# Zeros on GpSimd, later loads, and alternating products of r in an attention and expert kernel

## Chip, cores and metric

The kernel runs on one core of a Trainium2 chip. The metric is the time of one execution on the device in microseconds (us), as the median of several runs.

## The reference

First a recurrence over 768 steps for 4 x 8 heads of width 40, then an elementwise product of two projections with a third projection behind it:

```python
for t in range(S):
    y[:, :, t] = np.einsum('bhd,bhde->bhe', rt, state)
    Sa = np.einsum('bhde,bhe->bhd', state, at)
    state_decay = state * wt[:, :, None, :] - np.einsum('bhd,bhe->bhde', Sa, bt)
    state = state_decay + np.einsum('bhd,bhe->bhde', vt, kt)
...
a = x @ w_a        # 3072 x 320 by 320 x 1536
b = x @ w_b
return (a * b @ w_out).astype(np.float32)
```

The weights of the second part come as 64-bit floats, so the kernel decodes their words into a high and a low 32-bit part.

## The kernel before

The 768 steps are cut into 12 chunks n of 64 steps; each chunk has two halves c of the heads, numbered q = 2n + c. The stages of attention are:

- **Preparation** (`prep`, L512) of one q: loads of W, BK and A; two scans on VectorE (DVE), Q and pe, with a reciprocal between them; BK and A are multiplied by them; `scores` on TensorE (PE, L564), whose results go to AB (copied by ScalarE, ACT) and through a mask to TK (DVE); transposes of BK (`nat`, L599); and stores of A, pe, TK and bkn to a scratch tensor un_d in DRAM.
- **Lanes** (`lanes`, L611) for a pair of chunks, six times: a DVE transpose of AB into N, 31 dependent pairs of DVE instructions on Y that invert 32 x 32 triangles, and two transposes out, TC and T3.
- **Merge** (`merge`, L643) of one chunk: two rounds of 32 x 32 products (l2a, l2b) that complete the inverse T.
- **Main** (`main`, L696) of one q: loads of un (from un_d), SV and rv; the products r (`r_`, L721), u, s, g and y in a chain through ACT and DVE. The state ST runs from s of one chunk to r of the next, so this chain is serial over the chunks. r has 16 products: 128 rows deep, 64 stationary columns, 40 moving ones, written to one of two halves of the output's partitions (`half(j)`). s (`s_`, L757) has 16 of the same depth and moving width, with 40 stationary columns, and changes the half with each product.

The second part is cut into 12 slices of the 1536 inner columns. A **unit** (L416) is one slice times one chunk's 256 tokens: sixteen products into ab, a copy by ACT to asb, a product g by DVE, the split of g into gh (ACT) and gl (GpSimd, POOL), and six products into po. Four slices (F1) are worked while attention runs, eight after it. Each slice needs three weight pieces; a piece is loaded to one of two buffers wraw, decoded by six DVE, two ACT and two POOL instructions (L333), and written to a slot.

All instructions of this part are first recorded by a planner (`Plan`, L77) as operations with an engine, a cost, the keys that they read and write, and a due time v. `Plan.run` (L118) then walks through time and, on the engine that can start earliest, takes the ready operation that is due first. What it emits is kept in that order on each engine's queue: the keys set the order, while real waits come from the data. All DMAs are issued by SP, one queue in program order, with eight outstanding at most. Before the change the weights' loads read no key and the loads of SV and rv in `main` neither, so they are ready at time 0.

Ahead of the plan, L497 and L498 set zeros on DVE in AB, the two T, the two ST, the two RH and D1. tmp (L491) takes the sum of s and the old state before the decay is multiplied into ST.

Of the kernel before, what the change touches and what calls it, by code (L numbers as in the profile page):

```python
# [32 lines left out]
CW = M * CP  # L33
F1 = 4
# [31 lines left out]
class Op:  # L66
    __slots__ = ("eng", "dur", "fn", "deps", "users", "v", "lat", "need", "free", "mode", "end", "left", "ready", "seq", "moved")


class Banks:  # L70


    def __init__(self, n):
        self.n, self.ids = n, None


class Plan:  # L77
# [8 lines left out]
    def op(self, eng, dur, fn, r=(), w=(), v=None, lat=0.07, need=None, free=(), mode=None, moved=0.0):  # L86
        o = Op()
        o.moved = moved
# [29 lines left out]
    def run(self, slack=0.05, switch=0.13):  # L118
# [3 lines left out]
        last_mode = None  # L122
        ready = {e: [] for e in engines}
# [8 lines left out]
        while todo:  # L132
# [29 lines left out]
            if o.eng == "PE":  # L162
                if o.mode != last_mode:
                    d += switch
                last_mode = o.mode
            engines[o.eng] = s + d
# [94 lines left out]
def wkv_moe(ctx, tc, wd, ai, bk, rvf, vn, pin, rv, wa, wb, wo, out):  # L261
# [23 lines left out]

    def transp(ps, x):
        nc.tensor.matmul(ps, lhsT=x, rhs=ident, start=True, stop=True, is_transpose=True)
# [29 lines left out]
    pl = Plan(4)  # L317

    def us(n, fixed=0.16, each=0.00106):
        return fixed + each * n  # L320

# [9 lines left out]
    temps = [[stage.tile([P, NG * P], I32, name=f"w_{x}{i}") for x in ("ex", "mt", "rs")] for i in range(2)]  # L331

    def decode(i, src, rows, ncol, dst_hi, dst_lo, split):  # L333
# [3 lines left out]
        ex, mt, rs = (x[:rows, 0:ncol] for x in temps[i % 2])  # L337
# [4 lines left out]
        K, kr = [("w", i % 2, x) for x in ("ex", "mt", "rs")], ("raw", i % NR)  # L342
# [56 lines left out]
    def plan_tile(f, w, slot, v):  # L399
        for i, j, (eng, dur, fn, r, wr, lat) in tile_steps(f, w):  # L400
# [5 lines left out]
            pl.op(eng, dur, fn, r, wr, v=v, **kw)  # L406
# [6 lines left out]
          for x in ("asb", "g", "gh", "gl")}  # L413
    nunit = 0

    def unit(xk, kx, w, slot, first, last, done, v):  # L416
# [4 lines left out]
        ab, (asb, g, gh, gl) = AB2[i], (mo[x][i] for x in ("asb", "g", "gh", "gl"))  # L421
# [8 lines left out]
        for j in range(2):  # L430
            pl.op("PE", 0.95, lambda j=j: half(j), [kx] + wk, [("ab", i)], v=v, mode="r", lat=0.1)
# [7 lines left out]
        def second():  # L439
            for hf in range(2):  # L440
# [7 lines left out]
              v=v - 0.2, mode="r", lat=0.1)  # L448
# [18 lines left out]
    TK_ = ring(pp, 1, [P, 2, 4, C], "TK")  # L467
    PE_ = ring(pp, 2, [P, M, CP], "pe")
    BN_ = ring(pp, 1, [P, M, 2, D], "bkn")
# [21 lines left out]
    tmp = a1.tile([P, 4, 2, D], F32, name="tmp")  # L491
# [5 lines left out]
    for t in (AB, *T_, *ST_, *RH_, D1):  # L497
        nc0.vector.memset(t, 0.0)  # L498
# [13 lines left out]
    def prep(n, c, v):  # L512
        q = n * NP + c
        s2, x = q % 2, place[n]
        W, Q, BK, A, TK, PEt, BN = W_[s2], Q_[s2], BK_[s2], A_[s2], TK_[0], PE_[s2], BN_[0]
        kW, kQ, kBK, kA, kTK, kPE, kBN = ("W", s2), ("Q", s2), ("BK", s2), ("A", s2), ("tk", 0), ("pe", s2), ("bn", 0)
# [16 lines left out]
        pl.op("DVE", us(2 * M * C), lambda: nc.vector.tensor_mul(  # L533
# [7 lines left out]
        pl.op("DVE", us(M * C), lambda: nc.vector.tensor_mul(out=A, in0=A, in1=PEt[:, :, 0:C]), [kPE], [kA])  # L541
# [31 lines left out]
        pl.op("PE", 1.15, scores, [kBK, kA], need=ps, mode="q", lat=0.1, w=[("sc", q), kAB, kTK])  # L573
# [22 lines left out]
        for k in range(2):  # L596
# [8 lines left out]
            pl.op("PE", 0.5, nat, [kBK], need=ps, mode="t", lat=0.1, w=[("nt", q, k), (*kBN, k)])  # L605
# [37 lines left out]
    def merge(n, x, v):  # L643
# [25 lines left out]
        pl.op("PE", 1.15, l2a, kab + [("T3", x)], [("l3", n), "W4"], need=ps, mode="h", lat=0.1)  # L669
# [13 lines left out]
        pl.op("PE", 1.15, l2b, ["W4", ("TC", x)], [("l4", n), kT[2]], need=ps, mode="h", lat=0.1)  # L683
# [6 lines left out]

    def load_v(n, c, v):

        pl.dma(lambda: nc.sync.dma_start(out=SV_[c].rearrange("p g j i d -> p (g j i d)"), in_=vn[n, c]),
               [], [("svv", c), ("svs", c)], 1.1, v=v)
# [530 lines left out]
```

## Time and profile before

| | |
|---|---|
| three timed runs | 881.32, 872.25, 878.12 us; median 878.12 |
| the profiled execution | 881.76 us; span 879.8 us; mean granted TensorE clock 0.911 |
| busy share of the span | PE 83%, PE's weight loads 78%, DVE 68%, ACT 43%, POOL 26% |
| first transpose into N; last G of attention | 63.84 us; about 573 us |
| DMA | 156.58 MB, mean 178 GB/s |

In the page's slices each digit is the busy share of a fortieth of the span (22 us) in tenths. The chain of waits goes back from the last instruction to what released it, so its shares tell which engine the time was spent on when everything else waited. A window row sums busy time within a stretch. Nearly all instructions carry the line of one helper, L60, so groups are told apart by tile: "at<-SV,un 128*64 128x40" is the product r (128 rows, 64 stationary columns, 40 moving), "128*40" is s, "at<-A,BK" are the scores, "ab<-xk,wt" and "po<-wo" the unit's products, and w_ex, w_mt and w_rs the decode. PE shows two instructions for each fp32 product, so r has 32.

### The profile page before, as it was taken

Reading aid. Unit: us, or ns where it says so; the run is one execution under the profiler, and the core shown is the slowest. Engines: PE = TensorE matmul, PEld = TensorE weight load, DVE = VectorE, ACT = ScalarE, POOL = GpSimd, SP = SyncE. Lnnn points to the kernel's source line nnn. Section 1 sums busy time; section 2 is a strip of 40 time slices with the busy share of each in tenths; the row PEclk is TensorE's granted clock in tenths of the full one; section 3 lists DMA queues with packets and bytes.
Section 4 is the critical chain, followed back from the end, with each engine's and each line's share of the span. In section 5 each row is a group of like instructions: output and inputs, shape, how many; then the busy total and the mean of one; then the engine's idle time right before and its main releaser. Section 6 shows DMA issues by size and latency. Waiting matters only on the chain.

```text
span 879.8 us, 29127 instructions
## 1 busy us (share of the span) xinstructions
PE 728.7 (83%) x12538; PEld 684.8 (78%) x12538; DVE 594.3 (68%) x1162; ACT 379.8 (43%) x991; POOL 232.2 (26%) x265
## 2 busy tenths in 40 slices
PE   2453577788897898897989997799699999999996
PEld 2342466788787787787869886699699999999996
DVE  8979878969798798978658534874499822222222
ACT  3452473466535564644644453443244422222221
POOL 1310000244312011211112122455266622222222
PEclk9997588859996899989988999799899999999999
DMA  7897389768977878987775769579522100000111
GB/s 262 291 298 236 90 251 366 208 187 276 285 231 180 262 242 283 262 272 248 213 234 161 231 200 254 154 206 222 131 81 71 40 1 2 1 1 2 60 60 64
DMA packets 102018, 156.58 MB, mean 178 GB/s; under 512 B 30250, under 2 KB 70250, under 8 KB 98810
## 3 DMA queue, kind: packets, MB, share of 16 engines
q1 hardware_dynamic: 101882, 154.64, 58.3%
q8 instruction: 100, 1.64, 0.8%
q14 instruction: 36, 0.29, 0.1%
HBM read 101.97 MB, written 48.78 MB: 171 GB/s over the span
## 4 chain that ended last, share of the span: by engine, by line
PE 49%; DVE 26%; DMA 11%; issue 9%; ACT 3%; POOL 1%; SPq 0%; DVEq 0%; ACTq 0%; POOLq 0%
PE ab L60 20%; PE at L60 19%; PE po L60 9%; DVE Yt L60 5%; DVE Y L60 4%; DMA wraw<-in_wb_dram 3%; DVE w_ex L60 2%; DMA xk<-xk_d 2%; DVE w_mt L60 2%; DVE g L60 2%; DVE pe L60 1%; DVE w_rs L60 1%; DVE Q L60 1%; DMA wraw<-in_wa_dram 1%; DVE G L60 1%
## 5 line engine op out<-in xcount | busy, mean ns | idle before, releaser
L60 PE MATMUL ab<-xk,wt 120*128 120x256 f32 x2304 | 314.8, 290 | 15.1 <-issue 7.8
L60 PEld LDWEIGHTS ab<-xk,wt 120*128 120x128 f32 x2304 | 297.2, 196 | 18.1 <-issue 8.3
L60 POOL TENSOR_TENSOR gl<-g,gh 128x256 fp32r<-128x256 f32 x144 | 115.9, 805 | 403.8 <-ACT gh L60 399.5
L60 DVE TENSOR_TENSOR g<-ab,asb 128x256 f32<-128x256 f32 x144 | 60.5, 421 | 181.5 <-ACT asb L60 181.3
L60 PE MATMUL po<-wo,gh 128*128 128x320 f32 x576 | 156.8, 322 | 8.1 <-ACT gh L60 7.4
L60 ACT COPY asb<-ab 128x256 f32<-128x256 f32 x144 | 53.5, 372 | 155.5 <-PE ab L60 155.2
L60 PEld LDWEIGHTS po<-wo,gh 128*128 128x128 f32 x576 | 105.5, 194 | 11.0 <-ACT gh L60 8.4
L60 PE MATMUL po<-wo,gl 128*128 128x320 f32 x288 | 92.6, 322 | 3.2 <-POOL gl L60 3.2
L60 ACT CAST gh<-g 128x256 fp32r<-128x256 f32 x144 | 58.4, 406 | 78.4 <-DVE g L60 77.3
L60 PE MATMUL at<-SV,un 128*64 128x40 f32 (+1 forms) x1472 | 70.2, 232 | 15.8 <-ACT w_ex L60 4.6
L60 PEld LDWEIGHTS at<-SV,un 128*64 128x64 f32 (+1 forms) x1472 | 64.2, 142 | 23.1 <-ACT w_ex L60 5.0
L60 DVE TENSOR_TENSOR Y<-Y,Yt 128x31 f32<-128x31 f32 (+15 forms) x186 | 68.4, 368 | 6.4
L60 DVE TENSOR_TENSOR Yt<-Y,N 128x31 f32<-128x31 f32 (+15 forms) x186 | 67.7, 364 | 4.9
L60 PE MATMUL at<-ident,BK 128*128 128x128 f32 x192 | 36.0, 338 | 34.7 <-DMA rv<-in_rvf_dram 14.1
L60 PEld LDWEIGHTS po<-wo,gl 128*128 128x128 f32 x288 | 56.2, 195 | 6.2 <-POOL gl L60 5.8
L60 PEld LDWEIGHTS at<-ident,BK 128*128 128x128 f32 x192 | 27.2, 173 | 37.7 <-issue 19.6
L60 POOL TENSOR_TENSOR xk<-XF,xk 120x512 fp32r<-120x512 f32 (+1 forms) x24 | 34.1, 1443 | 65.0 <-ACT xk L60 64.6
L60 POOL TENSOR_TENSOR w_mt<-w_mt,wt 120x384 f32<-120x384 f32 x24 | 26.3, 1095 | 79.8 <-ACT wt L60 79.7
L60 PE MATMUL at<-A,BK 64*64 64x64 f32 x1536 | 38.2, 270 | 9.2 <-ACT bkn L60 6.8
L60 PEld LDWEIGHTS at<-A,BK 64*64 64x64 f32 x1536 | 34.5, 180 | 14.0 <-ACT bkn L60 8.4
L60 PE MATMUL at<-T,AB 32*32 32x32 f32 x768 | 18.6, 210 | 31.4 <-DVE T L60 26.1
L60 DVE TENSOR_TENSOR acc<-po,acc 128x320 f32<-128x320 f32 x96 | 42.3, 481 | 2.7 <-PE po L60 2.7
(84 smaller groups left out, 1131.1 us busy)
## 6 DMA issues: line engine op xcount, KB each, us to landing
un<-un_d SPq DMA_DIRECT2D x24, 1092.0 KB
BK<-in_bk_dram SPq DMA_DIRECT2D x24, 512.0 KB
rv<-in_rvf_dram SPq DMA_DIRECT2D x24, 512.0 KB
xk_d<-xk SPq DMA_DIRECT2D x11, 720.0 KB
xk<-xk_d SPq DMA_DIRECT2D x11, 720.0 KB
SV<-in_vn_dram SPq DMA_DIRECT2D x24, 320.0 KB
un_d<-bkn SPq DMA_DIRECT2D x24, 320.0 KB
W<-in_wd_dram SPq DMA_DIRECT2D x24, 260.5 KB
```

The source lines that it names most:

```text
L60: r = fn(*args, **kwargs)
```

## The change

- AB is not set to zero any more. The zeros of T, ST and RH are set by POOL, those of D1 stay on DVE.
- The weights' loads read a planner key that the second q's scores write (`WG`), and the first four slices are recorded behind the preparation and the lanes of the first pair. The loads of un, SV and rv for chunk 0 read the key N (`begun`), so they come behind the first transpose into N in the planner's time.
- r loops over i and gq outside and j inside, so that its products alternate between the two halves of the output.
- The planner gets a model of PE's clock: a 3.413 us window with less than 5100 columns of work makes the next one 1.85 times as long (`Clock`), and each PE operation gets its `work`. It moves instructions, and does nothing on the chip by itself.
- g takes the place of asb, and ST that of tmp.
- Of new settings NTK, NBN, NTMP, FILLERS and ON_POOL keep what was there before (one TK, one bkn, two sets of decode temporaries, no filler products, nothing of the preparation on POOL). One product with zeros into unused columns of PO, with its cast and its zeros on DVE, is new at the start.

```diff
+CLK, FILL, FILLC = 1, 0.6, 0.9
+WG = [("sc", 1)]
...
+class Clock:
+    WINDOW, ENOUGH, SLOW = 3.413, 5100, 1.85
...
+    def full(self, t):
+        return self.work.get(int(t / self.WINDOW) - 1, 0.0) >= self.ENOUGH
...
+                    d = clock.run(s, d, o.work) - s
...
+    fl = const.tile([P, P], F32R, name="fl")
+    nc0.vector.tensor_copy(out=fl, in_=ident)
+    fr = const.tile([P, 192], F32R, name="fr")
+    nc0.vector.memset(fr.bitcast(F32), 0.0)
...
+    mul(PO[0][:, 320:512], fl, fr)
...
-            pl.op(eng, dur, fn, r, wr, v=v, **kw)
+            pl.op(eng, dur, fn, list(r) + (WG if eng == "SP" else []), wr, v=v, **kw)
...
-        pl.op("ACT", 0.37, lambda: nc.scalar.copy(out=asb, in_=ab[:, 0, :]), [("ab", i)], [("asb", i)], v=v - 0.4)
-        pl.op("DVE", 0.42, lambda: nc.vector.tensor_mul(out=g, in0=ab[:, 1, :], in1=asb),
-              [("ab", i), ("asb", i)], [("g", i)], v=v - 0.4)
+        pl.op("ACT", 0.37, lambda: nc.scalar.copy(out=g, in_=ab[:, 0, :]), [("ab", i)], [("g", i)], v=v - 0.4)
+        pl.op("DVE", 0.42, lambda: nc.vector.tensor_mul(out=g, in0=ab[:, 1, :], in1=g),
+              [("ab", i)], [("g", i)], v=v - 0.4)
...
-    for t in (AB, *T_, *ST_, *RH_, D1):
-        nc0.vector.memset(t, 0.0)
+    nc0.vector.memset(D1, 0.0)
+    for t in (*T_, *ST_, *RH_):
+        nc0.gpsimd.memset(t, 0.0)
...
+    def begun(n):
+        return ["N"] if n == 0 else []
...
-        pl.dma(lambda: nc.sync.dma_start(out=UN, in_=un_d[q]), [("un", q, i) for i in range(5)], [kU], 3.7, v=v - 0.3)
+        pl.dma(lambda: nc.sync.dma_start(out=UN, in_=un_d[q]), [("un", q, i) for i in range(5)] + begun(n), [kU], 3.7, v=v - 0.3)
...
-            out=RV.rearrange("p x m t -> p (x m t)"), in_=rvf[n, c]), [], [kRV], 1.7, v=v - 0.2)
+            out=RV.rearrange("p x m t -> p (x m t)"), in_=rvf[n, c]), begun(n), [kRV], 1.7, v=v - 0.2)
...
-            for j in range(2):
-                for i in range(4):
-                    for gq in range(2):
+            for i in range(4):
+                for gq in range(2):
+                    for j in range(2):
                         k = mi(gq, i) * D
                         mul(bank(ps)[half(j), k:k + D], AK[:, gq, j, i], SV[:, gq, j, i])
...
-    for f in range(F1):
-        plan_tile(f, slots[f], f, wv[f])
...
+        if g[0] == 0:
+            for f in range(F1):
+                plan_tile(f, slots[f], f, wv[f])
```

The order on the engines moves with this. SP's queue behind the loads of the first two q, before the change (the digit behind a tile's name is its buffer, the last number only a running one):

```order
L60 DMA SV0_206<-in_vn_dram 128x640
L60 DMA rv0_208<-in_rvf_dram 128x1024
L60 DMA SV1_207<-in_vn_dram 128x640
L60 DMA rv1_209<-in_rvf_dram 128x1024
L60 DMA wraw0_159<-in_wa_dram 120x768
L60 DMA wraw1_160<-in_wb_dram 120x768
L60 DMA un_d0_126<-pe0_192 128x520
L60 DMA W0_181<-in_wd_dram 128x521
L60 DMA un_d0_126<-A0_189 64x2x256 x2
L60 DMA un_d0_126<-bkn0_194 128x640
L60 DMA BK0_187<-in_bk_dram 128x1024
L60 DMA un_d0_126<-TK0_191 64x2x256 x2
```

and with the change:

```order
L66 DMA un_d0_131<-pe0_195 128x520
L66 DMA W0_184<-in_wd_dram 128x521
L66 DMA un_d0_131<-A0_192 64x2x256 x2
L66 DMA A0_192<-in_ai_dram 128x512
L66 DMA un_d1_132<-pe1_196 128x520
L66 DMA BK0_190<-in_bk_dram 128x1024
L66 DMA un_d0_131<-TK0_194 64x2x256 x2
L66 DMA un_d0_131<-bkn0_197 128x640
L66 DMA un_d1_132<-A1_193 64x2x256 x2
L66 DMA W1_185<-in_wd_dram 128x521
L66 DMA un_d2_133<-pe0_195 128x520
L66 DMA un_d2_133<-A0_192 64x2x256 x2
```

The loads of chunk 0's SV and rv and the first two weight pieces have left the place behind the first six loads; the preparation's own stores and loads have moved up to it.

PE's queue around the first r, which before stood between the second and the third scores:

```order
L60 MATMUL at3_66<-ident_71,BK0_187 128x128 x4
L60 MATMUL at2_65<-ident_71,BK0_187 128x128 x4
L60 MATMUL at2_65<-SV0_206,un0_202 64x40 x16
L60 MATMUL at2_65<-A0_189,BK0_187 64x64 x2
L60 MATMUL at3_66<-A0_189,BK0_187 64x64 x2
L60 MATMUL at2_65<-A0_189,BK0_187 64x64 x2
```

With the change both r of chunk 0 stand behind the transposes that follow the fifth scores:

```order
L66 MATMUL at0_63<-ident_71,BK0_190 128x128 x4
L66 MATMUL at1_64<-ident_71,BK0_190 128x128 x4
L66 MATMUL at1_64<-SV0_209,un0_205 64x40 x16
L66 MATMUL at1_64<-SV1_210,un1_206 64x40 x16
L66 MATMUL at1_64<-A1_193,BK1_191 64x64 x2
L66 MATMUL at0_63<-A1_193,BK1_191 64x64 x2
```

The two r now follow each other and stand ahead of the sixth scores instead of ahead of the third and the fourth.

DVE's queue from the end of the first round of lanes, before:

```order
L60 STREAM_TRANSPOSE TC_199<-Y_197 128x32x32
L60 STREAM_TRANSPOSE T3_200<-Y_197 128x32x32
L60 SCALAR_TENSOR_TENSOR Q1_184<-W1_182,one_76 128x521
L60 TENSOR_TENSOR BK1_188<-BK1_188,Q1_184 128x1024
L60 TENSOR_SCALAR rp_186<-Q1_184 128x8
L60 RECIPROCAL d1_185<-rp_186 128x8
L60 SCALAR_TENSOR_TENSOR pe1_193<-W1_182,d1_185 128x520
L60 TENSOR_TENSOR A1_190<-A1_190,pe1_193 128x512
L60 TENSOR_SCALAR w_ex1_164<-wraw1_160 128x320
L60 TENSOR_SCALAR w_mt1_165<-wraw1_160 128x320
L60 TENSOR_SCALAR w_rs1_166<-wraw1_160 128x320
L60 SCALAR_TENSOR_TENSOR Q0_183<-W0_181,one_76 128x521
```

and with the change:

```order
L66 STREAM_TRANSPOSE TC_202<-Y_200 128x32x32
L66 STREAM_TRANSPOSE T3_203<-Y_200 128x32x32
L66 SCALAR_TENSOR_TENSOR Q1_187<-W1_185,one_81 128x521
L66 TENSOR_TENSOR BK1_191<-BK1_191,Q1_187 128x1024
L66 TENSOR_TENSOR TK0_194<-at2_65,tri_84 128x512
L66 TENSOR_SCALAR rp_189<-Q1_187 128x8
L66 RECIPROCAL d1_188<-rp_189 128x8
L66 SCALAR_TENSOR_TENSOR pe1_196<-W1_185,d1_188 128x520
L66 TENSOR_TENSOR A1_193<-A1_193,pe1_196 128x512
L66 SCALAR_TENSOR_TENSOR w_rs1_171<-w_rs1_171,w_ex1_169 120x384
L66 TENSOR_SCALAR w_ex0_166<-wraw0_164 128x320
L66 TENSOR_SCALAR w_mt0_167<-wraw0_164 128x320
```

Ahead of the first transpose into N stand 30 decode instructions before the change and 11 with it; behind the first round, up to the second transpose into N, four pieces and the end of another stand where there was one.

More of the change, by code (lines that the diff above doesn't have):

```diff
@@ L66 @@
 class Op:
-    __slots__ = ("eng", "dur", "fn", "deps", "users", "v", "lat", "need", "free", "mode", "end", "left", "ready", "seq", "moved")
+    __slots__ = ("eng", "dur", "fn", "deps", "users", "v", "lat", "need", "free", "mode", "end", "left", "ready", "seq", "moved", "work")
 class Banks:
@@ L74, in __init__, with run @@
         self.n, self.ids = n, None
+class Clock:
+    WINDOW, ENOUGH, SLOW = 3.413, 5100, 1.85
+    def __init__(self):
+        self.work = {}
+    def full(self, t):
+        return self.work.get(int(t / self.WINDOW) - 1, 0.0) >= self.ENOUGH
+    def run(self, t, d, work):
+        left = 1.0
+        while left > 1e-9:
+            k = int(t / self.WINDOW)
+            d1 = d if self.full(t) else d * self.SLOW
+            part = min(left, ((k + 1) * self.WINDOW - t + 1e-9) / d1)
+            self.work[k] = self.work.get(k, 0.0) + part * work
+            t += part * d1
+            left -= part
+        return t
 class Plan:
@@ L122, in run @@
         last_mode = None
+        clock = Clock()
         ready = {e: [] for e in engines}
@@ L165, in run @@
                 last_mode = o.mode
+                if CLK:
+                    t = engines["PE"]
+                    if self.filler and s - t > 0.4:
+                        share = FILL if clock.full(t) else FILLC
+                        nf = int(share * (s - t) / (0.09 if clock.full(t) else 0.17))
+                        for _ in range(nf):
+                            self.filler()
+                            t = clock.run(t, 0.09, 384)
+                        self.nfill = getattr(self, "nfill", 0) + nf
+                        s = max(s, t)
+                    d = clock.run(s, d, o.work) - s
             engines[o.eng] = s + d
@@ L412, in wkv_moe @@
     mo = {x: [mp.tile([P, 256], F32R if x in ("gh", "gl") else F32, name=f"{x}{i}") for i in range(2)]
-          for x in ("asb", "g", "gh", "gl")}
+          for x in ("g", "gh", "gl")}
     nunit = 0
@@ L420, in unit @@
         nunit += 1
-        ab, (asb, g, gh, gl) = AB2[i], (mo[x][i] for x in ("asb", "g", "gh", "gl"))
+        ab, (g, gh, gl) = AB2[i], (mo[x][i] for x in ("g", "gh", "gl"))
         wt, wot = w
@@ L762, in s_ @@
                             mul(bank(ps)[hd(j), c0:c0 + D], BN[:, mi(gq, i), j], SV[:, gq, j, i])
-            pl.op("PE", 0.75, s_, [kU, kS, kV], [("s", q), kST, "tmp"], need=ps, mode="c", lat=0.1)
+            pl.op("PE", 0.75, s_, [kU, kS, kV], [("s", q), kST], need=ps, work=2560, mode="c", lat=0.1)
             sv = ST[:, :, :, 0:D]
@@ L945, in wkv_moe @@
               + [(k, c) for k in ("svs", "svv", "rv", "rh", "st", "sd") for c in range(NP)]
-              + [("ut", 0), ("ut", 1), ("gm", 0), ("gm", 1), "tmp", ("x", 0)] + [("xf", 0, i) for i in range(3)])
+              + [("ut", 0), ("ut", 1), ("gm", 0), ("gm", 1), ("x", 0)] + [("xf", 0, i) for i in range(3)])
     def late():
@@ L1108, in all_tiles @@
             w = weight_tiles(p, "s")
[L1109 removed]
+            g, gh, gl = (mo[x][0] for x in ("g", "gh", "gl"))
             for f in range(NF):
@@ L1116, in all_tiles @@
                         mul(AB2[0][:, j, :], w[0][:, j, kw, :], xk[:, kxi, :], k == 0, k == 7)
-                nc.scalar.copy(out=asb, in_=AB2[0][:, 0, :])
-                nc.vector.tensor_mul(out=g, in0=AB2[0][:, 1, :], in1=asb)
+                nc.scalar.copy(out=g, in_=AB2[0][:, 0, :])
+                nc.vector.tensor_mul(out=g, in0=AB2[0][:, 1, :], in1=g)
                 nc.scalar.copy(out=gh, in_=g)
```

71 lines of the change are left out of this document (41 added, 30 removed).

## Prediction

> **What bounds the kernel now.** I read the page's slices first, then its chain of waits, then busy time by stage. The stage edges are events on VectorE (DVE): start of the first transpose into N, which opens the first round of lanes; end of the last transpose that closes it; the second transpose into N; the end of its round; the third transpose into N; the end of attention.
>
> ```profile
> PE   2453577788897898897989997799699999999996
> DVE  8979878969798798978658534874499822222222
> PE 49%; DVE 26%; DMA 11%; issue 9%; ACT 3%; POOL 1%; SPq 0%; DVEq 0%; ACTq 0%; POOLq 0%
> 0.00:63.80 63.80, 24.71 (x384) 21.82 (x388) 53.78 (x81) 26.04 (x66) 14.54 (x25) 1.00 0.86 282
> 63.80:98.00 34.20, 8.65 (x196) 7.16 (x189) 32.14 (x74) 8.74 (x20) 0.00 (x0) 0.70 0.56 178
> 98.00:128.10 30.10, 25.91 (x764) 23.34 (x764) 23.81 (x38) 21.44 (x59) 2.84 (x4) 0.67 0.69 196
> 128.10:165.20 37.10, 27.90 (x735) 24.54 (x734) 32.24 (x83) 16.24 (x45) 2.54 (x2) 0.90 0.91 316
> 165.20:228.10 62.90, 51.56 (x1196) 47.50 (x1194) 49.59 (x80) 33.46 (x88) 21.94 (x21) 0.76 0.79 234
> 228.10:573.00 344.90, 299.83 (x6983) 273.87 (x6981) 253.65 (x501) 174.50 (x468) 71.23 (x71) 0.90 0.77 231
> 573.00:879.80 306.80, 290.18 (x2300) 286.55 (x2300) 149.07 (x312) 99.37 (x247) 119.13 (x143) 0.98 0.25 67
> 63.84 2.07 DVE N L60
> 128.19 2.06 DVE N L60
> ```
>
> A window row gives its length, then busy time with instruction counts of PE, PE's weight loads, DVE, ACT, POOL, then the granted clock, the DMA share and GB/s. Three regimes stand there. Until 98 DVE is the limit: 53.78 of 63.80 us, then 32.14 of 34.20, with PE mostly waiting. From 98 to 573 PE and DVE share it: PE is busy 405 of 475 us, DVE 359, and each waits for the other. After 573 PE alone is full; those 306.8 us are units of the second half, whose order the change leaves nearly alone. So I look for gains ahead of 98 and in PE work of attention, and let the last stage move as a block.
>
> **The zeroing.** Before its first scan, DVE sets zeros:
>
> ```profile
> 1.74 3.47 DVE L498 MEMSET AB<- 128x4096 f32 x1 [1.74 <-PEq L1214]
> 5.37 0.91 DVE L498 MEMSET T<- 128x1024 f32 x1 [0.16 <-issue]
> 7.41 1.03 DVE L498 MEMSET ST<- 128x512 f32 x2
> 8.49 1.02 DVE L498 MEMSET RH<- 128x512 f32 x2
> 9.57 0.49 DVE L498 MEMSET d<- 128x520 f32 x1
> 9.98 1.18 DVE L60 TENSOR_TENSOR_SCAN Q<-W,one 128x521 f32<-128x521 f32 x1
> 1.28 4.39 DMA BK<-in_bk_dram
> 2.87 1.16 POOL L60 MEMSET Y<- 128x1024 f32 x2
> ```
>
> AB's zeros vanish, those of T (two tiles), ST and RH go to POOL: 3.47 + 2 x 0.91 + 1.03 + 1.02 = 7.3 us leave DVE. The first scan then waits for W's load, which was issued ahead of the BK load that ended at 1.28 + 4.39 = 5.67, or for the constant `one` on POOL, now behind two zeroings of about 1 us each (Y's pair with the same 1024 columns took 1.16). I put the scan at 4.5 (bounds 4.0 and 5.7) instead of 9.98: 5.5 us won. The new matmul, cast and 192-column zeros stand in DVE's and PE's idle first 4 us; without that cover they would cost well under the 0.49 of d's zeros. POOL's 4 us of zeros lie ahead of its first decode work, which now comes later still: nothing.
>
> **The loads and weights held back.**
>
> ```profile
> 9.98:63.80 53.82, 46.14 (x74) 1.00 0.87 281
> L60 DVE SCALAR_TENSOR_TENSOR w_ex<-wraw,w_ex 120x384 int32<-120x384 int32 (+1 forms) x5 | 3.9, 782 | 2.6 <-ACT w_ex L60 2.6
> L60 DVE TENSOR_TENSOR w_mt<-w_ex,w_mt 120x384 int32<-120x384 int32 (+1 forms) x5 | 3.4, 675 | 0.1
> L60 DVE TENSOR_TENSOR TK<-at,tri 128x512 f32<-128x512 f32 x4 | 2.7, 686 | 4.3 <-PE at L60 4.3
> L60 DVE SCALAR_TENSOR_TENSOR w_rs<-w_rs,w_ex 120x384 f32<-120x384 int32 (+1 forms) x5 | 2.7, 537 | 0.0
> L60 DVE TENSOR_SCALAR w_mt<-wraw 120x384 int32<-120x384 int32 (+1 forms) x5 | 1.7, 346 | 0.0
> L60 DVE TENSOR_SCALAR w_rs<-wraw 120x384 int32<-120x384 int32 (+1 forms) x5 | 1.7, 345 | 0.0
> L60 DVE TENSOR_SCALAR w_ex<-wraw 120x384 int32<-120x384 int32 (+1 forms) x5 | 1.7, 340 | 0.0
> 52.73 3.22 PE at L60 x32
> ```
>
> The first row is DVE's busy time from the first scan to N, the next seven are groups in that stretch (busy, mean ns, idle before). Ahead of N stood 30 decode instructions; the order of the change has 11. The 19 that go are 3 each of the first two groups' kinds, 4 of w_rs<-w_rs, 3 of each tensor-scalar: 3 x 0.782 + 3 x 0.675 + 4 x 0.537 + 3 x (0.346 + 0.345 + 0.340) = 9.6 us. DVE idled 53.82 - 46.14 = 7.7 us there, 4.3 of it in TK's group behind PE. The chain shows why: the product r of the second half of chunk 0 (52.73, 3.22 us) stood in PE's queue ahead of the fourth scores and waited for its loads. Both r now stand behind the fourth scores, as the PE rows above show, and their loads behind DVE's lanes; what queues behind them is only preparation of chunks 2 and 3, which this N does not need. I leave 5 us of idle (bounds 2 and 8, since 0.87 of the DMA engines were busy). N then starts at 4.5 + 46.14 - 9.6 + 5 = 46 instead of 63.8: 17.8 us early.
>
> Most of that is borrowed. The 9.6 us of decode come after this round, in the two stretches up to the end of the second round, where DVE is busy 56 of 67 us. I charge all of it: 17.8 - 9.6 = **8.2 us** stay. If the waits of PE in those stretches hid the decode entirely, 17.8 would stay; if N came no earlier than bounds of 5.7 and 8 us allow, 4. SP's queue is the risk: the first weight piece that finds its buffer still in use stops every preparation load behind it. The order has only one such piece (the third) ahead of the last load that N waits for.
>
> **The products of r.**
>
> ```profile
> L60 PE MATMUL at<-SV,un 128*64 128x40 f32 x768 | 48.5, 240 | 12.5 <-ACT w_ex L60 4.6 <-ACT bkn L60 3.3 <-DVE X L60 2.9
> L60 PE MATMUL at<-SV,un 128*40 128x40 f32 x704 | 22.0, 223 | 3.3 <-ACT SV L60 1.4 <-DVE rp L60 1.1 <-ACT uT L60 0.8
> 133.70:135.80 2.10, 1.92 (x32) 0.92 1.05 379
> 148.40:150.40 2.00, 1.85 (x32) 1.00 0.98 334
> 118.40:119.40 1.00, 0.81 (x32) 1.00 0.68 204
> 215.94 1.16 PE L60 MATMUL at<-A,BK 64*64 64x64 f32 x64 [1.07 <-DVE A L60]
> 133.84 1.93 PE at L60 x32
> 540.21 2.46 PE at L60 x60
> ```
>
> The first group is r (24 times 32 instructions), the second s, which has the same depth and moving width but already alternates between the output halves. One r takes 1.92 or 1.85 us (third and fourth rows, PE busy), one s 0.81 (fifth). The scores with r's 64 weight columns spread over four quarters of the array: 64 instructions in 1.16 us (sixth), which over two halves at the same pace per quarter is 1.16 for r's 32. So the new r lies between 0.81 and 1.16; I take 1.0, so 0.85 us less than the quicker r. In all 24: about 21 us of PE. But only r that stand in the chain of waits count: after the first round these are 11, the first at 133.84 and the last inside the piece at 540.21. That is 11 x 0.85, and one of them I found as slow as that at 52.73, and it gives 1.5: **10 us**. Bounds: 0, if DVE's lanes become the longer path each time, and 24 x 1.04 + 2 = 27 if PE is the limit throughout.
>
> Here two pages of the Trainium skill differ. "TensorEngine Tiling (Array Packing)", Tiling Modes, has different tiles load weights and multiply in parallel. "TensorE: Matmul & The Clock Gate", Part 3, lets weight loads overlap only when the row group differs, and r's two halves share all rows. By the first the sum keeps its 10 us, by the second it loses them, which is the first rival; the s row bears out the first.
>
> **Shared buffers.** asb gives way to g, so ACT's next copy waits for POOL's gl of two units before.
>
> ```profile
> L60 POOL TENSOR_TENSOR gl<-g,gh 128x256 fp32r<-128x256 f32 x144 | 115.9, 805 | 403.8 <-ACT gh L60 399.5
> 273.50 3.71 PE ab L60 x16
> 706.91 1.92 PE ab L60 x16
> ```
>
> The first products of two units alone last 2 x 1.92 = 3.8 us (third row) and gl 0.805, so it is free in time; uncovered it could cost at most gl per unit. tmp's going is the same work in place.
>
> **The sum.** 881.76 (profiled execution; its span 879.8) - 8.2 - 10 = 863.6. The three timed runs have a median of 878.12, 3.6 below the profiled one, so I predict 860.
>
> **Rivals.**
> (a) r's overlap does not come, or DVE hides it: only 8.2 stay, 870. For it: DVE is busy 80% of the middle. Against: s, and eleven r in the chain.
> (b) Both pay in full: 17.8 + 17 (two thirds of r's upper bound, PE being 85% busy) leave 843. For it: PE's idle share; against: DVE as the next limit.
> (c) Slower, through PE's clock. The planner now spreads units by its own clock model, and shorter r leave PE more gaps. A unit's sixteen first products take 3.71 us at the low clock (273.50) and 1.92 at the full one: 1.8 us each. From 11 of attention's 42 units on that now run slow, the 18 us are gone; at 17 the time is 890. For it: granted clocks of 0.67 and 0.76 in two stages; against: r's gaps are under 1 us each, and many units run slow already.
> (d) The new order costs about what it saves: 876. For it: every queue is rearranged; against: DVE's groups keep their sequence, round by round.
>
> **Chances.** Forecast (853 to 867) 0.48, (a) 0.17, (b) 0.18, (c) 0.09, (d) 0.08. A measurement of this kernel can tell about 1% from no change, here 869.3. Faster by over 1%: the forecast, (b) and some two fifths of (a), 0.73; within 1%: the rest of (a) and (d), 0.18; slower 0.09. The range, 842 to 878, holds (a), (d) and most of (b).
>
> **What would show it.** The first scan before 6 us; N before 51; the round closed before 85; the second N 8 to 14 us early; r's group at 20 to 29 us of busy time instead of 48.5, with its weight loads shorter too; attention's end 13 to 25 us early; the last stage within 3 us of 306.8. Wrong would be an N after 58, r above 40 us, or a clock under 0.85 between 228 and 573 where 0.90 stood.

## The result: 0.9% faster, and the profile after

| | before | after |
|---|---|---|
| median of the timed runs | 878.61 us (20 runs, 872.25 to 886.46) | 870.43 us (20 runs, 862.77 to 877.48) |
| ratio, 95% interval | | 0.9911 [0.9889, 0.9932] |
| profiled execution; span; mean granted clock | 881.76; 879.8; 0.911 | 869.84; 868.0; 0.883 |
| start of the first and second transposes into N | 63.84; 128.19 | 49.07; 117.74 |
| end of the last G of attention | 573.21 | 556.54 |
| from there to the end of the span | 306.6 | 311.5 |

The change is faster by 8.2 us; the forecast was 18. The slices and the chain of the page after:

```profile
PE   3335856778887979997988997599799999999996
DVE  7799888999996888688689225843799733323332
PE 40%; DVE 27%; DMA 20%; issue 6%; ACT 3%; SPq 2%; POOL 2%; DVEq 0%; POOLq 0%; ACTq 0%
```

PE's share of the chain fell from 49 to 40%, transfers rose from 11 to 20%. Five of the stretches of the prediction (columns: length, PE, weight loads, DVE, ACT, POOL with counts, granted clock, DMA share, GB/s), the last one from 573 to the end:

```profile
0.00:63.80 63.80, 21.91 (x393) 17.20 (x393) 53.66 (x89) 25.27 (x66) 10.16 (x24) 0.65 0.85 280
63.80:98.00 34.20, 20.42 (x465) 18.02 (x467) 31.33 (x61) 16.60 (x39) 6.42 (x7) 0.50 0.70 203
98.00:128.10 30.10, 19.55 (x551) 17.43 (x546) 26.32 (x52) 17.19 (x47) 4.41 (x5) 0.73 0.68 220
228.10:573.00 344.90, 294.56 (x7021) 266.88 (x7021) 249.93 (x509) 175.94 (x472) 70.85 (x76) 0.92 0.77 233
573.00:868.00 295.00, 279.78 (x2157) 276.20 (x2156) 137.61 (x288) 92.15 (x231) 113.45 (x136) 0.98 0.22 63
```

The work stands earlier: from 63.8 to 98 PE does 465 instructions, before 196. What else answers to the rows of before, first DVE's start, the transposes into N, and the last G:

```profile
1.20 0.49 DVE L554 MEMSET d<- 128x520 f32 x1
3.74 1.24 DVE L66 TENSOR_TENSOR_SCAN Q<-W,one 128x521 f32<-128x521 f32 x1
49.07 2.15 DVE L66 STREAM_TRANSPOSE N<-AB 128x1024 f32<-128x1024 f32 x1
117.74 2.17 DVE L66 STREAM_TRANSPOSE N<-AB 128x1024 f32<-128x1024 f32 x1
555.26 1.28 DVE L66 TENSOR_TENSOR G<-at,tri 128x512 f32<-128x512 f32 x2
```

Then r and its weight loads (groups by form: busy us, mean ns):

```profile
L66 PE MATMUL at<-SV,un 128*64 128x40 f32 x768 | 29.7, 240 | 18.1 <-DMA SV<-in_vn_dram 10.1 <-DMA un<-un_d 3.5 <-DVE X L66 2.5
L66 PEld LDWEIGHTS at<-SV,un 128*64 128x64 f32 x768 | 26.9, 148 | 21.7 <-issue 11.2 <-DMA un_d<-A 3.7 <-DVE X L66 2.9
417.20 1.13 PE L66 MATMUL at<-SV,un 128*64 128x40 f32 x32
```

Each instruction of r still takes 240 ns, but they follow each other more closely: 1.13 us for 32 instead of 1.85, which I read as the two halves overlapping.

**How far one profile carries.** Both kernels were profiled a second time (k2 and j2 below). Up to 268 us their stage edges repeat within 2.6 us; at attention's end the kernel before gave 573.21 and 568.82. The ratios leave out executions over 1.5% above the fastest of the same kernel, so that they can differ from the ratio of two medians, and the second profile of the change fell in such an execution (881.58 us against a median of 871.27), so its late edges aren't used. Ends of the other single profiles lie up to 8 us from their kernel's median. So leads are read from profiles, and gains at the end from medians. In the expectations below "attention's end" (or last G) counts to the first G of the last chunk (544.26 before, 529.43 after), a stage edge earlier than that of the table.

### The profile page after: what moved, and what is told of

The parts are those of the page before. It is cut to its first block, busy times and chain, and to the rows that moved or that the text cites. A ratio compares the mean times of both kernels' runs of the same rounds, so it can differ in the third digit from the quotient of the medians.

```text
span 868.0 us, 29180 instructions
## 1 busy us (share of the span) xinstructions
PE 712.9 (82%) x12539; PEld 665.1 (77%) x12539; DVE 589.7 (68%) x1157; ACT 379.1 (44%) x991; POOL 233.9 (27%) x271
## 4 chain that ended last, share of the span: by engine, by line
PE 40%; DVE 27%; DMA 20%; issue 6%; ACT 3%; SPq 2%; POOL 2%; DVEq 0%; POOLq 0%; ACTq 0%
PE ab L66 19%; PE at L66 12%; PE po L66 9%; DMA wraw<-in_wb_dram 4%; DVE Yt L66 4%; DVE Y L66 4%; DVE w_ex L66 3%; DMA BK<-in_bk_dram 2%; DVE w_mt L66 2%; DVE w_rs L66 2%; SPq L66 2%; DMA xk<-xk_d 2%; DMA XF<-x_d 2%; DMA wraw<-in_wo_dram 2%; DMA SV<-in_vn_dram 2%
## 5 line engine op out<-in xcount | busy, mean ns | idle before, releaser
L66 PE MATMUL ab<-xk,wt 120*128 120x256 f32 x2304 | 320.2, 292 | 11.9 <-DVE g L66 11.1
L66 PEld LDWEIGHTS ab<-xk,wt 120*128 120x128 f32 x2304 | 301.7, 198 | 15.6 <-ACT wo L66 9.9
L66 DVE TENSOR_TENSOR g<-ab,g 128x256 f32<-128x256 f32 x144 | 60.5, 420 | 171.6 <-ACT g L66 171.4
L66 ACT COPY g<-ab 128x256 f32<-128x256 f32 x144 | 53.6, 372 | 184.0 <-PE ab L66 178.6
L66 DVE TENSOR_TENSOR Y<-Y,Yt 128x31 f32<-128x31 f32 (+15 forms) x186 | 72.4, 389 | 6.4
L66 DVE TENSOR_TENSOR Yt<-Y,N 128x31 f32<-128x31 f32 (+15 forms) x186 | 70.6, 380 | 4.6
L66 PE MATMUL at<-SV,un 128*64 128x40 f32 (+1 forms) x1472 | 51.2, 230 | 24.4 <-DMA SV<-in_vn_dram 10.1
L66 PEld LDWEIGHTS at<-SV,un 128*64 128x64 f32 (+1 forms) x1472 | 44.9, 140 | 32.5 <-issue 12.3
L66 PE MATMUL at<-ident,BK 128*128 128x128 f32 x192 | 38.4, 348 | 22.0 <-DVE TK L66 9.7
L66 PE MATMUL at<-rv,uT 64*64 64x64 f32 x768 | 34.7, 248 | 16.7 <-DVE ST L66 6.1
L66 PEld LDWEIGHTS at<-rv,uT 64*64 64x64 f32 x768 | 30.4, 159 | 19.8 <-DVE ST L66 6.4
```

Source lines behind the costliest of these rows:

```text
L66: r = fn(*args, **kwargs)
```

## Experiments

All ratios are to the kernel before, on the same chip.

### The parts in the order of before

Edits to the kernel before: e2 takes r's new loop order alone, e3 the zeros alone (AB's gone, the rest on POOL), e7 both.

```diff
-            for j in range(2):
-                for i in range(4):
-                    for gq in range(2):
+            for i in range(4):
+                for gq in range(2):
+                    for j in range(2):
```

> The kernel before, with only the loop order of r changed; the order on every engine is that of before. Each r gets 0.72 us shorter (1.85 to 1.13). Theory A and C: 11 r in the chain, so 8 us or more: ratio 0.988 to 0.992. Theory B: 0.996 to 1.000.

> The kernel before, with only AB's zeros left out and those of T, ST and RH set by GpSimd; the order on every engine is otherwise that of before. The first scan comes at about 4 us instead of 10. Theory A: DVE bounds the first 98 us but the transfers (0.87 of the DMA engines busy) take part of it back: 2 to 4 us, ratio 0.995 to 0.998. Theory B and C: the whole 5.5 us stay: 0.992 to 0.995.

> The kernel before with the loop order of r and the place of the zeros changed, and nothing held back, no clock model: the order on every engine is that of before. Theory A: r 8 us and zeros 2 to 4: ratio 0.984 to 0.989, quicker than the whole change (0.991). Theory B: 0.990 to 0.994. Theory C: 0.982 to 0.986, since all of the loss is in the new order.

| run | ratio, 95% interval | first scan; N |
|---|---|---|
| e2, r alone | 1.0022 [0.9981, 1.0063] | 10.0; 63.2 |
| e3, zeros alone | 1.0014 [0.9974, 1.0055] | 3.7; 63.4 |
| e7, both | 0.9968 [0.9933, 1.0004] | 3.7; 62.8 |

None of the three ratios lies in a range that its theories gave; only for e7 is a gain likely, of some 0.3%, and its interval reaches 1. In e3 DVE begins 6.2 us earlier and N gains 0.4. DVE's rows of e3 ahead of N, then PE's (in brackets the idle time ahead and what ended it):

```profile
58.19 0.69 DVE L60 TENSOR_TENSOR TK<-at,tri 128x512 f32<-128x512 f32 x1 [5.92 <-PE at L60]
60.53 1.24 DVE L60 TENSOR_TENSOR_SCAN Q<-W,one 128x521 f32<-128x521 f32 x1
63.40 2.14 DVE L60 STREAM_TRANSPOSE N<-AB 128x1024 f32<-128x1024 f32 x1
```

```profile
52.38 3.20 PE L60 MATMUL at<-SV,un 128*64 128x40 f32 x32 [7.35 <-DMA un_d<-TK]
56.11 1.98 PE L60 MATMUL at<-A,BK 64*64 64x64 f32 x64 [0.53 <-ACT RH L60]
```

DVE waits for scores that stand in PE's queue behind r of the second half, and that r waits 7.35 us for transfers: it starts at 52.38, in the kernel before at 52.73. DVE's wait behind it is 5.92 us where it was 3.16; another 2.6 of the won time goes earlier, in waits for W (1.61) and for a store of TK (0.97) that the kernel before doesn't have. With the order of the change, where both r and their loads stand behind, the zeros do move N (next).

### The parts in the order of the change

Edits to the changed kernel: e1 and j1 (the same kernel twice) put r back in its old order, f1 puts all zeros back on DVE, AB's too, k1 does both, which leaves the order alone (with the shared buffers and the one product of zeros, which no run takes apart from it).

```diff
-    nc0.vector.memset(D1, 0.0)
-    for t in (*T_, *ST_, *RH_):
-        nc0.gpsimd.memset(t, 0.0)
+    for t in (AB, *T_, *ST_, *RH_, D1):
+        nc0.vector.memset(t, 0.0)
```

> The kernel after, with the products of r back in their old loop order (all of one half of the output, then all of the other); the order on every engine is that of the kernel after. Theory A (r pays on the chain of waits, and what was lost is the start, given back to transfers between 80 and 165 us): the ratio to before is 0.999 to 1.004, since r was nearly the whole gain. Theory B (r is mostly hidden, the start paid its 8 us): 0.990 to 0.994. Theory C (the planner's new order costs what the rest saves): 1.000 or above, up to 1.010. In all, r's group reads about 48 us of PE again instead of 29.

> The changed kernel with r alone in its old order, a second time, since its profile was the fastest of its twelve runs (872.38 against a median of 877.61). Theory, that r's alternation is worth 5 to 10 us at the end in the new order, about what the forecast gave it (10), and that it was the start's 8.2 that did not come: 0.996 to 1.003 of the kernel before, attention's end between 530 and 538. Rival, that the first measurement was off and r is worth nothing at the end: 0.989 to 0.993.

> The kernel after, with all zeros set by DVE again (AB's too); the order on every engine is otherwise that of the kernel after. With the zeros moved in the kernel before, the first scan came at 3.7 instead of 10.0 us, and N at 63.4 instead of 63.8: the fourth scores stood behind the product r, which waited for its loads. Theory D (DVE bounds the way to N once r and its loads stand behind N): the first scan at 10, N at 54 to 56 instead of 49.1, and the ratio to before is 0.995 to 0.999 instead of 0.991. Theory T (the transfers bound it, busy 0.98 between 20 and 40 us): N at 49 to 51 and the ratio stays at 0.990 to 0.993.

> The changed kernel with r in its old order and with all zeros, AB's too, set on DVE as before; what stays of the change is the order (held loads and weights, clock model, shared buffers). Theory: each of the two parts only pays because the others stand beside it, and their effects add up in the new order (without the zeros' part 1.41% longer, without r's 0.83%), so the order by itself is slower than the kernel before: 0.9911 x 1.0141 x 1.0084 = about 1.013, 890 us, with N at 55 and attention's end near 541. Rival: the parts stand in for each other (either one gives the chain its slack), so the order without both is no worse than without one: 0.999 to 1.006. A second rival, that the order alone made the gain, would give 0.99.

| run | zeros | r | ratio, 95% interval | median, us | N |
|---|---|---|---|---|---|
| k1 | old | old | 1.0014 [0.9974, 1.0054] | 880.33 | 55.1 |
| e1 | new | old | 0.9994 [0.9955, 1.0032] | 877.61 | 48.7 |
| j1 | new | old | 1.0010 [0.9977, 1.0043] | 878.57 | 48.4 |
| f1 | old | new | 1.0051 [0.9996, 1.0106] | 878.79 | 55.2 |
| the change | new | new | 0.9911 [0.9889, 0.9932] | 870.43 | 49.1 |

The order by itself gains nothing, though it moves N from 63.8 to 55.1. My theory for k1, effects that add up to 1.013, falls, and so does the reading that the order alone made the gain. Its number lies in the rival's range, but the rival's reason does not hold: if either part alone gave the chain its slack, e1 and f1 would have kept the gain. On top of the order, only both parts together pay. So what one part is worth depends on what stands beside it. With the new zeros in place r's loop order is worth 877.61 or 878.57 less 870.43, some 7 to 8 us; with the old ones (k1 to f1) nothing that can be told from noise. The zeros are likewise worth some 8 us beside the new r and nothing beside the old one. The loads held back make a third such part (e6, next).

### Where the early start goes: the second round of lanes

N comes 14.8 us early, the second N 10.4, the end of the second round (start of its TC, 165.2 before) only 2.7. Most of the loss is in the stretch between the last two: 44.8 us where it took 37.1 (42.8 and 37.2 in the second profiles). The chain of waits in that stretch, summed by line, of before:

```profile
by line: PE at L60 40.7%; issue 12.0%; DVE Yt L60 10.3%; DVE Y L60 9.6%; DVE G L60 5.6%; DVE N L60 5.6%; ACT SV L60 4.6%; DVE X L60 4.1%; DVE TK L60 3.5%; ACT RH L60 2.4%; ACT uT L60 1.8%; ACT SD L60 1.2%; DVEq L60 0.2%; DVE TC L60 0.1%
```

and of the change:

```profile
by line: PE at L66 24.1%; DMA un<-un_d 21.1%; DMA un_d<-TK 18.0%; DMA un_d<-A 12.0%; PE ab L66 7.0%; issue 6.9%; DVE TK L66 3.1%; DVE X L66 1.7%; DVE A L66 1.3%; SPq L66 1.3%; DVE Yt L66 1.2%; ACT SV L66 1.0%; ACT RH L66 1.0%; DVE g L66 0.9
```

Before, no transfer stands in this chain, in either profile; with the change transfers hold half of it. That suggests transfers as the reason, but the chain is not the same in all kernels of this order: by the same view transfers hold 41% of it in e1, 20% in j1 and nothing in f1, while the stretch takes 44.5, 46.4 and 43.2 us. What these kernels have in common is DVE: it is busy 38.3 us in the stretch of the change, and 38.1 to 38.4 in those of e1, j1, f1 and k1, where it was 32.2 before (32.1 in j2). That is 6.0 of the 7.7 us. Of the 6.0, 2.9 us are preparation of a further q (two scans, with rp and d between them), which before stood outside this stretch, and some 2.4 are three instructions on Y that took longer than the same ones before. Three lines of the change, and one of before:

```profile
121.95 1.24 DVE L66 TENSOR_TENSOR_SCAN Q<-W,one 128x521 f32<-128x521 f32 x1 [0.52 <-DMA W<-in_wd_dram]
123.67 1.24 DVE L66 TENSOR_TENSOR_SCAN pe<-W,d 128x520 f32<-128x520 f32 x1
149.38 1.35 DVE L66 TENSOR_TENSOR Y<-Y,Yt 128x220 f32<-128x220 f32 x1
```

```profile
154.47 0.39 DVE L60 TENSOR_TENSOR Y<-Y,Yt 128x220 f32<-128x220 f32 x1
```

Three kernels ask further. f2 leaves out the DVE decode of the first four slices (its output lacks it), f3 loads only 128 columns of each of their weight pieces (its output lacks the rest), e6 undoes the holding back; in f2 and f3, as in h1 below, POOL also sets zeros at the start in the tiles that are then not written:

```diff
+            if eng == "DVE":
+                fn = lambda: None
```

```diff
-            out=raw.rearrange("p c x -> p (c x)"), in_=src.bitcast(I32)), (), (kr,), 1.2
+            out=raw.rearrange("p c x -> p (c x)")[:, 0:128 if light else 2 * ncol],
+            in_=src.bitcast(I32)[:, 0:128 if light else 2 * ncol]), (), (kr,), 1.2
```

```diff
-WG = [("sc", 1)]
+WG = []
...
-        return ["N"] if n == 0 else []
+        return []
```

> The kernel after, with the DVE instructions of the decode of the first four slices left out (72 instructions, about 36 us of DVE; the weights of these slices are then zeros); everything else in its order. Theory D (the lead at N, 14.7 us, goes to DVE, which has 12 us more to do up to the end of the second round): that round ends 10 to 14 us earlier, at 149 to 153 us instead of 162.5, and attention ends earlier by 15 or more. Theory T (transfers between 80 and 165 us take it): the round ends within 4 us of 162.5.

> The kernel after, with the loads of the first four slices' weights cut to a sixth of their bytes (some 3.5 MB less before 210 us; the decode runs in full, on zeros mostly); everything else in its order. Theory T: N comes at 46 or earlier and the second round ends at 150 to 157 instead of 162.5. Theory D: N within 1.5 us of 49.1, the round's end within 3 us of 162.5.

> The kernel after, with nothing held back (weights planned first, chunk 0's loads ready at time 0); clock model, r and zeros as in the kernel after. If the held-back loads are what makes the zeros pay (moving them is worth nothing in the order of before and 6 us or more in that of after), N comes at 58 to 64 us and the ratio is 0.996 to 1.002. If the clock model does it, N comes at 49 to 53 and the ratio stays at 0.989 to 0.994.

f2: 0.9907 [0.9873, 0.9941], as the change. Its three stretches from N to the end of the second round:

```profile
49.20:79.00 29.80, 12.21 (x244) 10.30 (x239) 27.70 (x71) 6.35 (x16) 0.00 (x0) 0.61 0.75 263
79.00:117.00 38.00, 25.78 (x703) 23.14 (x704) 24.27 (x31) 26.58 (x68) 12.62 (x11) 0.63 0.78 221
117.00:160.50 43.50, 28.90 (x786) 25.74 (x785) 37.97 (x89) 16.47 (x45) 3.38 (x3) 0.77 0.86 300
```

```profile
78.90:117.70 38.80, 26.45 (x703) 23.73 (x704) 34.22 (x55) 26.81 (x68) 10.83 (x11) 0.59 0.75 216
117.70:162.50 44.80, 29.41 (x785) 26.42 (x784) 38.26 (x88) 16.66 (x45) 3.54 (x3) 0.77 0.87 289
```

Against the change (second fence) DVE has 10 us less to do in the middle stretch, 24.27 for 34.22, and the stretch is 0.8 us shorter. The decode is hidden there. f3: 0.9913 [0.9864, 0.9962]; its second N comes 3.5 us earlier, the round after it still takes 43.2 us and ends at 157.5, between what the two theories said, and nothing is left at the end. With lighter loads of un (h1, below) the stretch takes 42.9 us, and no transfer stands in its chain.

e6: 1.0000 [0.9964, 1.0035]. N falls back to 58.5, but the second round takes 39.2 us, and its chain has one transfer of another kind (xk_d<-xk, 11.8%):

```profile
118.93:158.14 39.21, 30.04 (x880) 25.86 (x879) 35.73 (x88) 17.57 (x48) 2.61 (x2) 0.86 0.95 309
```

Holding back is thus worth 9 us at N and costs 4 to 6 in the second round. That its transfers were pushed together there does not show: the DMA engines are busier in e6 (0.95) than in the change (0.87), and h1, which moves fewer bytes there (229 GB/s against 289), is no nearer to 37 us than f3. DVE's busy time does go with the length here, 35.7 us in e6. But no run takes the 6.0 us out of the change's DVE, and e3 took 42.8 us in this stretch with 32.8 of DVE, so that DVE's work is the cause is read from the rows and not tested. At the end holding back is worth 0.9%, though e6 reaches the end of the second round at 158.1, ahead of the change's 162.5. A lead there is not what sets the end. Without any one of three parts, r, the zeros or the holding back, nothing of the gain is left (e1 and j1, f1, e6).

### What sets attention's pace

Three kernels on the changed one: h1 loads 128 columns of un instead of all, h2 does two of eight pairs of unit products in the first four slices (both outputs lack the rest), k3 does r's products four times over.

```diff
-        pl.dma(lambda: nc.sync.dma_start(out=UN, in_=un_d[q]),
+        pl.dma(lambda: nc.sync.dma_start(out=UN[:, 0:128], in_=un_d[q][:, 0:128]),
```

```diff
+                if few and 0 < k < 7:
+                    continue
```

```diff
+            for again in range(4):
```

> The kernel after, with the loads of un cut to 128 of 2184 columns (24 MB less over attention; the rest of un is zeros, so the state is no longer the reference's); every engine in the order of the kernel after. Neither 36 us less of DVE decode nor the lighter weights moved the end, so something else sets attention's pace. Theory T (transfers): the last G comes 25 us or more earlier than the 529 us of the kernel after, and the ratio is 0.96 or less. Theory P (PE with its clock, and the chain of products and copies): the last G moves by less than 12 us, ratio 0.977 to 0.991.

> The kernel after, with two of eight products in each half of the units that run during attention (44 units, 528 products of some 0.12 us at the full clock, about 63 us of PE less; the sums are not the reference's); every engine in the order of the kernel after. Theory P: the last G comes 20 to 50 us earlier. Theory T: under 10 us, and r's saving of 18 us of PE could not show either. If both this and the lighter un move little, the serial chain from r to the state bounds, and r, which stands in it, should have shown.

> The changed kernel with the sixteen products of each r done four times over (same output, same order of all instructions): 3 x 1.13 = 3.4 us more PE for each r, 24 of them, 81 us more PE in all. Theory, that r lies in the slack of attention's chain through DVE and the transfers, so that halving it gave back little: of 3.4 us each a good part is hidden, 81 us of PE cost under 30 us, under 3.5% over the changed kernel. Rival, the prediction's own step: 11 of the 24 r lie in the chain of waits, so 11 x 3.4 = 37 us, ratio about 1.035 to the kernel before. If PE bounds attention throughout: 75 to 81 us, ratio 1.08.

h1: 0.9886 [0.9831, 0.9940]; h2: 0.9895 [0.9842, 0.9948]; neither can be told from the change's 0.9911. The stretch from 165 to 530, of the change and of h2:

```profile
165.00:530.00 365.00, 315.38 (x7962) 284.40 (x7958) 283.60 (x547) 197.91 (x535) 77.15 (x78) 0.92 0.80 244
```

```profile
165.00:530.00 365.00, 285.67 (x7428) 248.84 (x7428) 277.77 (x545) 195.53 (x528) 77.05 (x76) 0.84 0.81 241
```

With 534 matmuls fewer PE is busy 30 us less, where the expectation had 63, and the granted clock falls from 0.92 to 0.84. The Trainium skill, "TensorE: Matmul & The Clock Gate", Part 1, has activity release the throttle; the two rows agree, and it would explain why 30 us went and not 63. The last G comes 1.1 us earlier than with the change in h2, and 2.3 in h1: neither the transfers of un nor PE's products of units set the pace alone. For that case h2's expectation named the serial chain from r to the state, where r should show, and it does:

k3: 1.0457 [1.0403, 1.0511], 921.45 us. Its r:

```profile
L66 PE MATMUL at<-SV,un 128*64 128x40 f32 x3072 | 104.4, 239 | 19.8 <-DMA SV<-in_vn_dram 6.6 <-issue 4.5 <-DMA un<-un_d 4.0
```

104.4 - 29.7 = 74.7 us more of r cost 921.45 - 870.43 = 51.0 us: two thirds, more than my theory (under 30) and more than the forecast's share of the r in the chain (37), less than all. Lengthening r is dearer than shortening it pays: in e1 and j1 48.5 - 29.7 = 18.8 us of r were worth 7 to 8, two fifths. That a shorter r soon meets the next wait would explain it, but no run shows that wait.

### The clock model and two TK

e5 sets CLK = 0, g1 sets NTK = 2, g3 both.

```diff
-NTK, NBN = 1, 1
+NTK, NBN = 2, 1
...
-CLK, FILL, FILLC = 1, 0.6, 0.9
+CLK, FILL, FILLC = 0, 0.6, 0.9
```

> The kernel after, with the planner's clock model switched off; loads held back, zeros on GpSimd, r alternating as in the kernel after. If the new order's worth in the middle (e1, with the old r, had the second round's end to the last G 10 us shorter than before) comes from the clock model, the ratio is 0.997 to 1.003. If it comes from the loads held back, or if it is r's, the ratio stays at 0.988 to 0.994.

> The kernel after, with two buffers TK instead of one (the setting NTK). In the chain of the kernel after, DVE waits 8 us near 140 us for the store of the only TK, and SP waits behind it. Theory T (the lead is lost to such waits on transfers): the second round ends at 152 to 158 instead of 162.5, ratio 0.984 to 0.990. Theory P: the ratio stays at 0.989 to 0.994.

> The changed kernel with two buffers for TK and without the planner's clock model. Two TK alone gave 0.9886 with N at 42.3; leaving the clock model out gave 0.9952 with N at 45.4. Theory, that the start's lead is given back in the second round whatever its size: 0.988 to 0.996, N at 38 to 45, attention's end between 527 and 536. Rival, that a lead at N is kept: N some 9 us earlier than with the change, so 0.980 or less.

e5: 0.9952 [0.9913, 0.9991], between the two ranges of its expectation, so half of the gain may be the clock model's. g1: 0.9886 [0.9841, 0.9932], median 868.59; it beats the kernel before, but not the change by more than its interval. g3: 1.0012 [0.9972, 1.0052], outside both of its ranges. g1's second round ends at 160.9, not at 152 to 158. N stands at 45.4, 42.3 and 45.5: an early N again says little of the end, and two orders that do well apart do badly together.

### The last stage

The forecast let it move as a block. Its length, from the end of the last G to the end of the span, of before and its second profile j2, each in its own fence:

```profile
573.21:879.80 306.59, 290.18 (x2300) 286.55 (x2300) 148.86 (x312) 99.37 (x247) 118.92 (x143) 0.98 0.25 67
```

```profile
568.82:877.30 308.48, 291.27 (x2300) 287.75 (x2300) 148.48 (x312) 99.49 (x247) 118.70 (x143) 0.97 0.25 66
```

of the change, of j1 (r old), and of k1 (order alone):

```profile
556.54:868.00 311.46, 296.24 (x2319) 292.12 (x2318) 147.76 (x311) 99.57 (x248) 119.74 (x143) 0.98 0.23 65
```

```profile
561.82:875.30 313.48, 294.31 (x2319) 290.13 (x2318) 147.59 (x312) 99.43 (x248) 119.17 (x143) 0.97 0.24 65
```

```profile
561.33:876.10 314.77, 295.86 (x2319) 291.73 (x2318) 147.69 (x312) 99.61 (x248) 119.52 (x143) 0.97 0.25 65
```

and of e5 (no clock model):

```profile
560.21:864.40 304.19, 290.55 (x2301) 287.21 (x2300) 148.35 (x311) 99.24 (x247) 118.74 (x142) 0.98 0.24 67
```

The changed order leaves 2319 instructions of PE to this stage, before it were 2300: thirteen products into ab and six into po more, most of a unit, in a stage that PE fills. All five profiles in the order of before (with e2, e3, e7) lie between 305.4 and 308.9 us; those with 2319 instructions between 308.8 (f3) and 315.5 (h1), most of them between 313 and 315. At 290.18 us for 2300 the 19 instructions are 2.4 us (an estimate), half of the growth. The rest shows at the stage's start. Its first 15 us, of before and of the change:

```profile
573.21:588.21 15.00, 14.94 (x168) 14.60 (x169) 12.24 (x25) 7.62 (x18) 7.94 (x9) 1.00 0.64 193
```

```profile
556.54:571.54 15.00, 15.00 (x152) 14.46 (x152) 9.73 (x22) 6.45 (x15) 4.82 (x6) 0.83 0.44 120
```

PE is full in both, and in the change it does 16 instructions fewer, some 2 us, at a lower granted clock; all five profiles in the old order have 168 at 1.00, e1, j1, f1 and k1 153 to 162 at 0.84 to 0.92. e5, without the clock model, has 2301 instructions, 304.2 us, and 168 at 0.97. But g3, also without it, has 2319 and 311.8, so it is not the model by itself that leaves more behind. g1 puts the exchange most plainly: its last G ends at 546.30, 10 us ahead of the change, 2358 instructions are left, and the stage takes 319.1 us. Leaving the model out did not make the kernel faster, as e5's ratio says.

### Two controls

> The changed kernel itself, a second time, beside the others on the same chip. All theories: 0.989 to 0.993 of the kernel before. What it tells is how far one profile's stage edges repeat: if attention's end falls within 2 us of 529.4 and the last stage within 2 us of the first profile's 338.6 from attention's end to the end, differences of 5 us between kernels at the end of attention mean something; if they scatter by 5 us or more, those of single profiles do not.

> The kernel before itself, profiled a second time. All theories: 1.000 within 0.005. It tells how far its stage edges repeat: N at 63.8, the second round's end at 165.2 and attention's end at 544.3 within 3 us if the comparison of single profiles holds, and by how much the last edges scatter if not.

k2, the change again: 0.9874 [0.9826, 0.9922], a little below the range expected, median 871.27. j2, the kernel before again: 1.0062 [1.0012, 1.0111] to itself, though its medians, 879.68 and 878.55, are only 0.13% apart; its attention's end repeats within 3.6 us, not 3. A ratio from 8 runs can thus miss 1 by 0.6%; differences of that size between single experiments, as that of f1 to k1, are not proven. By its medians f1 is 1.0009. The change's gain rests on 26 runs of it and many more of before, and r's worth beside the new zeros on 24 runs without it.

## Why the prediction was wrong, step by step

**What held.** The first scan at 3.74 (forecast 4.5, below 6). The new cast took 2.06 us, and not well under 0.49, but it was covered as forecast: e3, which has no cast, begins its scan at 3.74 too. N at 49.1 (46; below 51): DVE's busy time from first scan to N fell by 8.4 us (46.14 to 37.77; 9.6 forecast), and 7.6 us of idle stayed, near the upper bound of 8, with 5.0 in the wait for W:

```profile
3.74:49.10 45.36, 16.89 (x329) 13.22 (x333) 37.77 (x55) 20.14 (x55) 7.06 (x14) 0.67 0.86 274
L66 DVE TENSOR_TENSOR_SCAN Q<-W,one 128x521 f32<-128x521 f32 x7 | 9.5, 1360 | 5.0 <-DMA W<-in_wd_dram 5.0
```

The first round closed from 78.9; the second N came 10.4 early (8 to 14). r's group has 29.7 us of busy time (just above the 20 to 29 forecast), 1.13 us each at full pace, near the scores' 1.16 and not at my 1.0. The Trainium skill's "TensorEngine Tiling (Array Packing)", Tiling Modes, agrees with that row; "TensorE: Matmul & The Clock Gate", Part 3, by which weight loads overlap products only when the row group differs, does not: r's halves share all rows, and its weight loads fell from 45.7 to 26.9 us. The clock between 228 and 573 stayed (0.92), so rival (c) did not come.

**The term for r** came out at the forecast's size in one place only: 10 us forecast, 7 to 8 measured in the new order beside the new zeros. In the order of before (e2) and beside the old zeros (k1 to f1) it was worth nothing.

**The step that failed** is the start's "8.2 us stay", with the sum that adds it to r's 10 as if each were paid by itself, and with "let the last stage move as a block". The start together with the new order, without r's part, gave 0.9994 and 1.0010: nothing within 3 us. r without the zeros gave nothing either, and without the loads held back both together gave 1.0000 (e6): the 8.2 us measured belong to the parts together. Of the working behind the 8.2, the 9.6 us charged for decode on DVE after the first round were wrong: f2 shows that the decode is hidden. The lead was lost there all the same, 14.8 us at N and 2.7 at the end of the second round. 7.7 of it went in the second round, which has 6.0 us more of DVE's busy time, none of it this decode.

This did not decide the end either. By the first profiles attention ended 573.21 - 556.54 = 16.7 us early, near the forecast's 18.2, but by luck: the lead was 2.7 us at the end of the second round, and e1, with the old r, ended at 556.52 too. Against the second profile of before it is 12.3. The last stage then gave back 311.5 - 306.6 = 4.9 us, in e1 and j1 over 6, where the forecast had at most 3. I had taken its length as given since its own order hardly changes; but the units that attention does not take are done there, PE is full there, and it starts at a lower clock.

**The sum of the miss.** Of the 18.2 us forecast 8.2 came, so 10.0 are missing. By the first profiles 1.5 of them are at attention's end and 4.9 in the last stage. The other 3.6 lie between the two profiled executions and the medians: that of before lay 3.2 us above the median of its 20 runs, that of the change 0.6 below. With the second profile of before, 5.9 would be missing at attention's end and 3.0 in the last stage, so this split is not settled; that the last stage grew rests on all the profiles of both orders.

**The rivals.** The time is that of rival (a), 870, but not for its reason: r's overlap did come, and the start without r was worth nothing. Rival (d), an order that costs what it saves, is nearer to what k1 shows.

**What stays open.** Why the zeros in the new order are worth nothing with the old r (k1 to e1) and some 8 us with the new one (f1 to the change), and r likewise. Single profiles do not show it: e1's attention ended at 556.52, as the change's. No kernel that I tried holds attention's products of units constant while the start moves, so how much of the last stage's growth comes from the shorter attention and how much from the planner's spreading stays open: e5 and g3, both without the clock model, point different ways. What the second round would take without the 6 us of DVE is not shown either.

## What to carry to other kernels

Where one stage's slack is filled with work from the next, a shorter first stage is paid for in the second: count what is left to do at the edge (here 2300 against 2319 instructions, half of the growth), and look at the clock with which the second begins, before treating the rest as a block. Price a part in the order in which it will stand and with its neighbours: r and the zeros were each worth nothing alone, in either order, and 8 us together in the new one. A chain of waits in one profile names a suspect; the same stretch in the other kernels of the order tells whether it was the cause. An early edge in a profile is a lead and no gain until the end is timed.

## What was not expected of the hardware

The granted clock of the first 100 us does not repeat between executions of one kernel: 0.50 and 0.91 stood for the same 29.8 us of the change, with PE busy 13.10 and 12.65 us:

```profile
49.07:78.87 29.80, 13.10 (x245) 10.88 (x240) 27.70 (x70) 6.35 (x16) 0.00 (x0) 0.50 0.71 247
```

```profile
49.70:79.50 29.80, 12.65 (x244) 10.59 (x240) 27.70 (x71) 6.36 (x16) 0.00 (x0) 0.91 0.73 263
```

So in a stretch where PE is mostly idle this column alone is no ground for an argument about its pace.
